# Attention with half-width key and query buffers, a new order of its steps, later weights, and the first layer's first two chunks taken together

## The chip, the cores and the metric

One NeuronCore of one Trainium2 chip runs the whole program in one launch. The metric is the device time in microseconds (us); lower is better. The engines are PE (TensorE matmul, with PEld for its weight loads), DVE (VectorE), ACT (ScalarE), POOL (GpSimd), and SP, which here only issues DMAs. TensorE's clock has two levels, 1.2 and 2.4 GHz; the profile gives the granted clock as a share of the upper one.

## What is computed

```
q, k, v: 4 batches x 8 heads x 576 tokens x 64
scores = q k^T / 8, a key block of 64 seen only by query blocks at or behind it
x   = softmax(scores) v          -> 2304 tokens x 512
x   = (s * relu(x w_in)^2 + b) w_out                 (d_ff 2048)
h   = max(x w1, x w2, x w3)                          (d_ff 768)
out = h w_out2
```

All in fp32; the weights arrive as 64-bit words and are turned into fp32 on the chip.

## The kernel before

The program has one function that records every operation with its reads, writes and a price per engine, and a planner (`Sched.run`) that then writes the instructions out in one fixed order per engine. What the planner puts behind what is settled at build time; on the chip each engine takes its list in order and waits at the head of it. `CFG` holds the tables that steer the planner: `order` (the steps of one round of attention), `pre` (how many weights are converted in each round), `off` (priorities by kind), `eng` (which engines may take a step), and the numbers of buffers.

**Attention** runs in 16 pairs of heads, each pair of one batch. For a pair `load_pair` brings keys and queries (one DMA of 1152 KB) and `load_values` the values. `prep_pair` makes the operands: high part of the keys (`khi`), of the queries (`qhi`), low parts (`klo`, and a fused step of L490), a scaled copy (`q2`), and small tiles for the first query block (`k0`). `softmax_pair` has nine units: scores on PE (full 128x128 array; the first unit on 64x64 tiles), a row maximum on DVE (L524), the exponential on ACT (L528). `values_pair` has five steps, each of which turns the weights of one key block on PE (transposes, L589), copies them out of PSUM on ACT (L389) and multiplies by the values on 128x64 tiles of the array. Round p does the scores of pair p, the values of pair p-1 and the operands of pair p+1. Raw keys and queries have two buffers, one in the tile `other` and one lent from the far end of the result tile `xf`; the staging buffers for weights are two plus two lent.

After the fourth, eighth, twelfth and sixteenth pair the reciprocals of the denominators go to DRAM and come back spread over the partitions (`normalize`, DMA of L796, multiplication of L800 on DVE).

**Weights.** One of w_in or w_out is 512 KB of words. `convert` takes four DVE operations (L694, L702, L706, L711) and one on ACT or POOL, `pair_out` one more on ACT or DVE and one subtraction on DVE (L394). The first half of the first layer's weights (16 tiles, `prepare_direct`) goes straight into SBUF; the others go to DRAM (`wscr`, `bscr`) and are fetched later. Of the 16, `pre` puts 11 into the rounds of attention.

**First layer.** 2304 tokens are cut in five chunks (three of 512, two of 384). A pass takes one chunk and 8 of the 16 blocks of d_ff: `l1` is 12 matmuls and five element steps that give h (relu, square, scale, high and low part), `l2` is 12 matmuls that add to four accumulators. Passes 0 to 4 use the first half of the weights, passes 5 to 9 the second half. The second layer follows.

In all of this a product of fp32 numbers is three matmuls on high and low parts, so one `l1` or `l2` of a block is 12 matmuls. The four lines that make the plan of the passes and of the first weights:

```
PASSES = [(0, c) for c in range(NC)] + [(1, c) for c in reversed(range(NC))]
order1 = [k for f_ in range(HF) for k in [("in", f_)] + [("out", f_ - 1)] * (f_ > 0)] + [("out", HF - 1)]
direct = order1[:8] + [k for k in order1[8:] if k[0] == "in"] + [k for k in order1[8:] if k[0] == "out"]
"pre": (0, 0, 0, 1, 1, 1, 1, 1, 1, 1, 1, 1, 1, 1)
```

Of the kernel before, what the change touches and what calls it, by code (L numbers as in the profile page):

```python
# [20 lines left out]
KT = DM // 128  # L21
# [77 lines left out]
class Ring:  # L99
    def __init__(self, aps):  # L100
        self.aps, self.last, self.n = aps, [None] * len(aps), 0

    def get(self):
        i = self.n % len(self.aps)
        self.n += 1
        u = Use(self.aps[i], [self.last[i]] if self.last[i] else [])
        self.last[i] = u
        return u


# [30 lines left out]


class Both:


    def __init__(self, own, lent):
        self.own, self.lent, self.i = own, lent, 0

    def get(self):
        self.i += 1  # L150
        n = len(self.own.at) + len(self.lent.aps)
        return (self.own if self.i % n < len(self.own.at) else self.lent).get()

    def close(self):

        gone, self.lent.aps = [u for u in self.lent.last if u], []
        for u in gone:
            u.over = True
        return [i for u in gone for i in u.ops]
# [23 lines left out]
class Sched:  # L183
# [45 lines left out]
    def run(self):  # L229
# [26 lines left out]
        while len(order) < n:  # L256
# [28 lines left out]
            if e == "PE":  # L285

                if side and not self.ops[i][5]:
                    c += 54
                side = self.ops[i][5] == "side"
# [11 lines left out]
def tile_attention_moe(ctx: ExitStack, tc: tile.TileContext, qk, vp, w_in, w_out, s_, b_, w123, w_out2, out):  # L301
# [13 lines left out]
    def places(at, n, *sizes):  # L315

        out_ = []
        for m, w in zip(n, sizes):
# [13 lines left out]
    SAT, NAT, at = places(0, (2, 2), 1024, 512)  # L332
    TAT = places(0, (5,), HN)[0]
    RAWAT, K0AT, NMAT, DENAT, RDAT, RVAT, PTAT, *EAT = places(at, (CFG["raw"], CFG["k0"], CFG["nmx"], 2, 1, CFG["rawv"], CFG["pt"]) + tuple(CFG["e"]),
                                                              2 * 2 * S, 256, NB, 36, 128, 17 * D, 1024, *e_w)
    FN = EAT.pop()
    RGAT1, PAT, SAT2, WV2, WB2, UAT, fn = places(at, (3, 4, 4, 2, 4, 6), 512, 512, 1024, 1024, 512, HN)
# [8 lines left out]
    wscr = dram.tile([2 * NF + NG, 128, 1024], F32, name="wscr")  # L346
    pscr = dram.tile([KT, 128, NT], F32, name="pscr")
# [12 lines left out]

    late = xf[:, :, 2 * S:]
    stages = [late[:, 3 - i, 0:1024].rearrange("p (c w) -> p c w", w=2) for i in range(CFG["lent"])]
    raws = [late[:, 0:2, :]] if CFG["lent"] == 2 else []

    def words2(t):
        return t.rearrange("p (c w) -> p c w", w=2)
    rings = dict(raw=Both(Strip(other, RAWAT, 4 * S, two), Ring(raws)), k0=Strip(other, K0AT, 256, lambda t: t[0:64]), nmx=Strip(other, NMAT, NB), den=Strip(other, DENAT, 36),
                 rdt=Strip(other, RDAT, 128), rawv=Strip(other, RVAT, 17 * D, lambda t: t.rearrange("p (a c) -> p a c", c=D)), pt=Strip(other, PTAT, 1024),
                 k1=Strip(arena, kq_at, 1152), q1=Strip(arena, [x + 1152 for x in kq_at], 1024, two), kq2=Strip(arena, [x + 2176 for x in kq_at], 2176),
                 x1=Strip(arena, XAT1, 1024, two), h1=Strip(arena, HAT1, 1024, two), iw=Strip(arena, IAT, 1024, two), ow=Strip(arena, OAT, 1024, two),  # L370
                 x=Strip(arena, XAT, 2 * HN, two), v=Strip(arena, VAT, 1024, two), h=Strip(arena, HAT + HATB, 2 * HN, two), w=Strip(arena, WAT_, 512, two),
                 wb=Strip(other, WB2, 512, two), wv=Strip(other, WV2, 1024, two),
                 stg=Both(Strip(other, SAT, 1024, words2), Ring(stages)), nrm=Strip(other, NAT, 512), rg1=Strip(other, RGAT1, 512), part=Strip(other, PAT, 512), t1=Strip(other, TAT[0:2], HN), t2=Strip(other, TAT[2:4], HN), tt=Strip(other, TAT[4:], HN), y=Strip(other, WV2, 512),
                 u=Strip(other, UAT, HN), rg=Strip(other, RGAT, HN), gb=Strip(other, GAT, HN),
                 **{"e%d" % j: Strip(other, EAT[j], w) for j, w in enumerate(e_w)})
# [23 lines left out]
    def load(size, f, eng="SP", **k):  # L399

        k["after"] = [op(eng, 380, f, lat=2000, **k)]
        return op("DMA", size / 330, lambda e: None, **k)
# [37 lines left out]
    def load_pair(p):  # L440
        b, hp = divmod(p, H // 2)
        R = rings["raw"].get()
# [8 lines left out]
        else:  # L451
            def f(e):
# [892 lines left out]
```

## Time and profile before

| what | value |
|---|---|
| median of 3 runs | 890.1 us (889.54 to 891.33) |
| the profiled execution, its own time | 888.34 us |
| its span, first to last instruction | 886.5 us |
| PE busy | 856.0 us (97%), 4802 matmuls |
| DVE busy | 624.0 us (70%) |
| ACT busy | 444.3 us (50%) |
| POOL busy | 92.6 us (10%) |
| DMA | 166.12 MB, mean 187 GB/s |
| mean granted TensorE clock | 0.985 |

Busy shares are means over stages with different limits: attention lasts to about 213 us, the first layer to about 600 us, the second to the end. Matmuls are pipelined, so a busy PE may still be waiting inside a matmul; the time from one matmul's start to the next tells more than the busy time.

### The profile page before, as it was taken

To read this page: it belongs to the slowest core of one execution; us is meant where nothing else is said; L and a number is where in the kernel's file an instruction comes from. 1 tells how busy PE (TensorE), PEld (TensorE's weight loads), DVE (VectorE), ACT (ScalarE), POOL (GpSimd) and SP (SyncE) were. 2 spreads that over 40 slices of the span, in tenths; PEclk is the share of its full clock that TensorE was granted. 3 is DMA by queue.
4 is the path that set the end of the run, shared out by engine and by line. 5 is a ranking of instruction groups with operands and counts; after the bars stand their busy time and mean duration, and the time that the engine had idled before them with its cause. 6 is when DMAs were issued, how large, how long until landed. Compare 5 with 4: busy or idle time off the path is not lost.

```text
span 886.5 us, 13632 instructions
## 1 busy us (share of the span) xinstructions
PE 856.0 (97%) x4802; PEld 740.7 (84%) x4802; DVE 624.0 (70%) x1211; ACT 444.3 (50%) x964; POOL 92.6 (10%) x96
## 2 busy tenths in 40 slices
PE   8899898889999999999999999999999999999997
PEld 7666565557788888999999888889999899989996
DVE  6898899887899999984734242546767666756662
ACT  5688887677577777764645343543013211331102
POOL 5332222210211031210000000000000000000000
PEclk9899999899999999999999999999999999999999
DMA  8454365554678988799311010126776477637641
GB/s 323 168 182 153 105 214 176 197 174 149 198 257 299 325 289 302 270 389 370 145 60 48 1 47 1 51 96 223 232 226 203 140 235 226 204 133 254 211 146 72
DMA packets 68755, 166.12 MB, mean 187 GB/s; under 512 B 8144, under 2 KB 12496, under 8 KB 67152
## 3 DMA queue, kind: packets, MB, share of 16 engines
q1 hardware_dynamic: 68000, 164.54, 54.9%
q8 instruction: 38, 0.62, 0.3%
q10 hardware_dynamic: 688, 0.72, 0.2%
q14 instruction: 29, 0.24, 0.1%
HBM read 127.67 MB, written 37.56 MB: 186 GB/s over the span
## 4 chain that ended last, share of the span: by engine, by line
PE 70%; DVE 13%; DMA 6%; ACT 6%; issue 3%; POOL 1%; SPq 0%; DVEq 0%; ACTq 0%; POOLq 0%
PE ps L397 67%; PE ps L589 3%; DMA other<-scr 3%; ACT other L528 3%; DVE arena L394 2%; DVE other L524 2%; DMA wscr<-other 2%; DVE other L711 2%; DVE other L394 2%; DVE other L706 1%; DMA bscr<-other 1%; POOL other L385 1%; ACT other L381 1%; DVE other L702 1%; DVE other L694 1%
## 5 line engine op out<-in xcount | busy, mean ns | idle before, releaser
L397 PE MATMUL ps<-arena 128*128 128x384 f32 (+6 forms) x3758 | 747.5, 357 | 9.3 <-ACT other L528 5.8
L397 PEld LDWEIGHTS ps<-arena 128*128 128x128 f32 (+1 forms) x3758 | 664.8, 190 | 85.4 <-issue 11.2
L882 DVE TENSOR_TENSOR other<-ps,other 128x384 f32<-128x384 f32 x189 | 101.0, 554 | 64.2 <-PE ps L397 62.4
L394 DVE TENSOR_TENSOR arena<-other,arena 128x384 fp32r<-128x384 f32 (+2 forms) x165 | 108.5, 665 | 18.9 <-ACT arena L381 14.8
L381 ACT ACTIVATE arena<-other 128x384 fp32r<-128x384 f32 (+4 forms) x105 | 61.1, 589 | 89.9 <-DVE other L1214 54.8
L931 ACT ACTIVATE other<-ps 128x512 f32<-128x512 f32 (+1 forms) x80 | 44.2, 552 | 116.1 <-PE ps L397 115.9
L383 DVE TENSOR_SCALAR arena<-other 128x512 fp32r<-128x512 f32 (+3 forms) x68 | 30.7, 452 | 94.8 <-ACT other L943 91.0
L528 ACT ACTIVATE other<-ps,other 128x320 f32<-128x320 f32 (+3 forms) x144 | 78.5, 552 | 33.2 <-DVE other L524 32.9
L389 ACT ACTIVATE other<-ps 128x512 f32<-128x512 f32 (+1 forms) x131 | 67.8, 559 | 29.1 <-PE ps L397 18.2
L524 DVE TENSOR_REDUCE other<-ps 128x1 f32<-128x320 f32 (+3 forms) x144 | 69.4, 513 | 15.0 <-PE ps L397 13.1
L589 PE MATMUL ps<-ident,other 128*128 128x128 f32 x400 | 64.6, 295 | 13.0 <-ACT other L528 6.7
L385 POOL TENSOR_SCALAR other<-other 128x512 f32<-128x512 f32 (+1 forms) x45 | 45.2, 1009 | 264.6 <-DVE other L694 170.3
L894 ACT ACTIVATE other<-ps 128x384 f32<-128x384 f32 x27 | 13.2, 490 | 114.9 <-PE ps L397 94.5
L397 PE MATMUL ps<-other 128*64 128x64 f32 (+5 forms) x640 | 66.7, 330 | 1.6 <-ACT other L389 1.6
L589 PEld LDWEIGHTS ps<-ident,other 128*128 128x128 f32 x400 | 47.2, 148 | 25.1 <-ACT other L528 10.5
L381 ACT ACTIVATE other<-other 128x256 fp32r<-128x256 f32 (+3 forms) x99 | 51.0, 524 | 29.3 <-DVE other L694 18.5
L943 ACT ACTIVATE other<-other,cst 128x512 f32<-128x512 f32 (+1 forms) x80 | 61.8, 772 | 2.0
L397 PEld LDWEIGHTS ps<-other 128*64 128x64 f32 (+1 forms) x640 | 30.2, 139 | 28.0 <-issue 16.1
L936 ACT ACTIVATE other<-other 128x512 f32<-128x512 f32 (+1 forms) x80 | 47.1, 589 | 2.1
L394 DVE TENSOR_TENSOR arena<-xf,arena 128x384 fp32r<-128x384 f32 (+4 forms) x61 | 40.5, 683 | 6.0 <-ACT arena L381 4.0
L394 DVE TENSOR_TENSOR other<-other 128x256 fp32r<-128x256 f32 (+1 forms) x85 | 41.8, 502 | 2.2 <-ACT other L381 1.8
L706 DVE SCALAR_TENSOR_TENSOR other<-other 128x512 uint32<-128x512 uint32 x54 | 39.2, 726 | 5.4 <-POOL other L385 3.3
(45 smaller groups left out, 360.2 us busy)
## 6 DMA issues: line engine op xcount, KB each, us to landing
arena<-bscr SPq DMA_DIRECT2D x189, 256.0 KB, 3.0
bscr<-other SPq DMA_DIRECT2D x63, 256.0 KB, 4.1
other<-qk SPq DMA_DIRECT2D x12, 1152.0 KB, 5.8
wscr<-other SPq DMA_DIRECT2D x22, 512.0 KB, 4.1
arena<-wscr SPq DMA_DIRECT2D x22, 512.0 KB, 5.0
other<-w_out SPq DMA_DIRECT2D x21, 512.0 KB, 5.4
other<-w SPq DMA_DIRECT2D x18, 512.0 KB, 5.5
other<-vp SPq DMA_DIRECT2D x16, 544.0 KB, 4.0
```

The costliest lines, as they stand in the source:

```text
L381: nc.scalar.activation(out=dst, in_=src, func=AF.Copy, scale=m)
L385: nc.gpsimd.tensor_scalar(out=dst, in0=src, scalar1=m, scalar2=1.0, op0=ALU.mult, op1=ALU.mult)
L389: nc.scalar.activation(out=dst, in_=src, func=AF.Copy)
L394: eng[e].tensor_tensor(out=dst, in0=a, in1=b, op=ALU.subtract)
L397: nc.tensor.matmul(o, l, r, start=start, stop=stop)
L524: nc.vector.tensor_reduce(out=NM.ap[:, u:u + 1], in_=v, axis=AX.X if n <= 512 else AX.XY, op=ALU.max, negate=True)
L528: nc.scalar.activation(out=ev, in_=v, func=AF.Exp, bias=NM.ap[:, u:u + 1], scale=1.0, accum_out=DEN.ap[:, d:d + 1])
L589: nc.tensor.transpose(TB.ap[:, 128 * i:128 * i + 128], x, ident)
L706: nc.vector.scalar_tensor_tensor(out=lo_w, in0=hi_w, scalar=3, in1=lo_w, op0=ALU.logical_shift_left, op1=ALU.bitwise_or)
L882: nc.vector.tensor_tensor(out=out_.ap, in0=bank.ap[:, 0:HN], in1=u.ap, op=ALU.add)
L936: nc.scalar.activation(out=r, in_=r, func=AF.Square)
L943: nc.scalar.activation(out=r, in_=r, func=AF.Identity, scale=s_t, bias=b_t)
```

## The change

- **Half buffers.** Keys and queries of a pair each get a buffer of half the width, four in all, in `other`, and a DMA of their own (576 KB). Nothing is lent from `xf` any more; weights have one staging buffer during attention, six after it.
- **A new order.** `values_pair` is split in two: the transposes with their copies (a to e) and the products (A to E). Products and the first score unit, which run on parts of the array, are collected and put out together where the order has a bar: two groups per round. Each of the five turned tiles has one buffer of its own. The planner is told 93 and 55 or 100 ns for a step between the full array and parts of it, where it was told 54 for one direction.
- **Engines.** `khi` and `qhi` go to POOL alone, `q2` to DVE alone, the copies of the result (`je`) to ACT alone. Loads and the normalization are given longer times in the plan.
- **Weights later.** Three weights instead of 11 are converted during attention (rounds 11 to 13); the w_in tiles come first, then the w_out tiles in the order 6, 7, 0 to 5.
- **First two chunks together.** `l1` runs for chunks 0 and 1 and all eight blocks first, then `l2` for both, with eight accumulators. h of blocks 0 to 5 (12 tiles of 512 KB) goes to DRAM (`hscr`) and comes back (`l1_back`). The passes then start at chunk 2.

```
-        R = rings["raw"].get()
+        R = [rings["raw"].get() for _ in range(2)]
...
-                nc.sync.dma_start(out=R.ap, in_=qk[b, hp])
-            load(1179648, f, writes=[(R, (i,) + k) for i in range(2) for k in ALL])
+                nc.sync.dma_start(out=R[i].ap, in_=qk[b, hp, :, i])
+                load(589824, f, lat=2000 if p < 3 else CFG["dlat"], writes=[(R[i], k) for k in ALL])
...
+    def side_by_side():
+        if side:
+            def f(e, fs=[x[1] for x in side]):
+                for g in fs:
+                    g(e)
+            op("PE", sum(x[0] for x in side), f, reads=[r for x in side for r in x[2]], writes=list(dict.fromkeys(w for x in side for w in x[3])),
+               kind="av", mode="side")
+            for g in after_side:
+                g()
...
-    PASSES = [(0, c) for c in range(NC)] + [(1, c) for c in reversed(range(NC))]
+    PASSES = [(0, c) for c in range(2, NC)] + [(1, c) for c in reversed(range(NC))]
...
+    late_ = [HF - 2, HF - 1] + list(range(HF - 2))
+    direct = [("in", f_) for f_ in range(HF)] + [("out", f_) for f_ in late_]
...
+    split_x(1, "x1b")
+    for f_ in range(HF):
+        while ("in", min(f_ + 2, HF - 1)) not in ready:
+            prepare_direct("w")
+        for c in range(2):
+            l1(c, f_, banks.get(SETS[0]), f_ < HF - 2)
+    accs[0, 0], accs[0, 1] = (accumulators(SETS[1 - c], KT) for c in range(2))
+    split_x(2)
+    for i, f_ in enumerate(late_):
+        while ("out", late_[min(i + 2, HF - 1)]) not in ready:
+            prepare_direct("w")
+        for c in range(2):
+            for k in range(KT):
+                l2(c, f_, k, accs[0, c], 0, i)
+        if i + 2 < HF:
+            for c in range(2):
+                l1_back(c, late_[i + 2])
...
-       "order": "1a5b7v06c3428dep",
+        'order': '2ba40AB7c6v|15dCeDEp8|3',
...
-       "pre": (0, 0, 0, 1, 1, 1, 1, 1, 1, 1, 1, 1, 1, 1),
+        'pre': (0, 0, 0, 0, 0, 0, 0, 0, 0, 0, 0, 1, 1, 1),
...
-       "nlat": 4000,
+        'nlat': 9000,
```

`l1_back` is one DMA from `hscr` into the next of the four h buffers.

Where rows move: PE in an early round of attention. Operations with `64x` are on parts of the array (`64x64 x2` first: the first score unit), `128x128` with `ident` are the transposes, the others with `arena` the scores. Before:

```order
L397 MATMUL ps<-other 64x512 x2
L397 MATMUL ps<-other 64x384 x2
L397 MATMUL ps<-other 64x64 x2
L397 MATMUL ps<-arena 128x448 x2
L589 MATMUL ps<-ident,other 128x128 x4
L397 MATMUL ps<-arena 128x320 x4
L397 MATMUL ps<-arena 128x192 x2
L397 MATMUL ps<-other 64x256 x2
L589 MATMUL ps<-ident,other 128x128 x3
L397 MATMUL ps<-arena 128x288 x4
L589 MATMUL ps<-ident,other 128x128 x4
```

and in the changed kernel:

```order
L367 MATMUL ps<-other 64x64 x2
L367 MATMUL ps<-other 64x512 x2
L367 MATMUL ps<-other 64x384 x2
L367 MATMUL ps<-arena 128x192 x2
L561 MATMUL ps<-ident,other 128x128 x7
L367 MATMUL ps<-arena 128x288 x4
L367 MATMUL ps<-arena 128x448 x2
L367 MATMUL ps<-arena 128x320 x2
L367 MATMUL ps<-other 64x256 x2
L367 MATMUL ps<-other 64x128 x2
L367 MATMUL ps<-other 64x64 x10
```

The products of 256, 128 and 64 columns, each on its own between full-array work before, now stand in one block; most rounds have exactly these two blocks.

DVE in the fifth round, before: two weights are under way (L694, L702, L706) among the maxima (L524) and the operands (L383, L394, L490).

```order
L694 TENSOR_SCALAR other<-other 128x512
L524 TENSOR_REDUCE other<-ps 128x1 x4
L702 TENSOR_SCALAR other<-other 128x512
L694 TENSOR_SCALAR xf<-xf 128x512
L706 SCALAR_TENSOR_TENSOR other<-other 128x512
L524 TENSOR_REDUCE other<-ps 128x1 x2
L383 TENSOR_SCALAR arena<-xf 128x1024
L391 COPY xf<-ps 128x64
L394 TENSOR_TENSOR arena<-xf,arena 64x1152
```

and in the changed kernel in a round as early (L353 is `q2`, L364 `klo`, L496 the maxima, L462 the fused step):

```order
L353 TENSOR_SCALAR arena<-other 64x1024
L364 TENSOR_TENSOR arena<-other,arena 64x1152
L496 TENSOR_REDUCE other<-ps 128x1
L462 SCALAR_TENSOR_TENSOR arena<-other,arena 64x1024
L496 TENSOR_REDUCE other<-ps 128x1 x8
```

The weights and the copies are gone from these rounds; nine maxima and three operand steps are left.

SP in the first layer of the changed kernel, where h comes back (L962) among loads of later weights (L680), the normalization (L786) and stores of converted weights (L722). The kernel before has no such rows.

```order
L962 DMA arena<-hscr 128x1024
L680 DMA other<-w_out 128x1024
L680 DMA other<-w_in 128x1024
L962 DMA arena<-hscr 128x1024
L786 DMA other<-scr 64x384 x2
L722 DMA wscr<-other 128x1024
L680 DMA other<-w_out 128x1024
L786 DMA other<-scr 64x384 x2
L962 DMA arena<-hscr 128x1024 x2
L722 DMA wscr<-other 128x1024
```

A return of h stands behind loads and stores that wait for DVE's conversions.

## Rows read from the trace of the kernel before

**Rows 1.** Busy time by stretch: us, then busy us (instructions) of each engine, clock, DMA.
```profile
79.00:213.30 134.30, 117.79 (x901) 79.11 (x900) 114.08 (x204) 101.86 (x286) 25.70 (x29) 0.95 0.50 168
240.00:880.00 640.00, 639.62 (x3262) 585.18 (x3262) 420.92 (x856) 267.14 (x481) 29.18 (x20) 1.00 0.57 190
```

**Rows 2.** PE in order of time (start, us, operation): marks of four rounds and the end.
```profile
20.03 1.49 PE L397 MATMUL ps<-other 64*64 64x64 f32 x8
...
36.97 1.99 PE L397 MATMUL ps<-other 128*64 128x512 f32 x12
...
208.45 2.15 PE L397 MATMUL ps<-other 128*64 128x512 f32 x12
...
213.21 0.96 PE L397 MATMUL ps<-arena 128*128 128x512 f32 x3
```

**Rows 3.** Busy time by stretch: three single rounds of attention, columns as in rows 1.
```profile
48.10:58.00 9.90, 9.90 (x84) 6.86 (x83) 9.52 (x17) 8.98 (x29) 4.28 (x4) 1.00 0.49 174
...
58.00:69.20 11.20, 11.20 (x95) 8.41 (x94) 10.81 (x18) 9.61 (x31) 4.75 (x5) 1.00 0.63 203
...
166.30:181.80 15.50, 14.49 (x95) 9.03 (x94) 11.54 (x23) 11.91 (x32) 2.93 (x4) 0.86 0.53 173
```

**Rows 4.** PE in order of time inside the first of these rounds.
```profile
54.44 0.66 PE L589 MATMUL ps<-ident,other 128*128 128x128 f32 x4
55.02 0.55 PE L397 MATMUL ps<-other 128*64 128x128 f32 x8
55.54 0.66 PE L589 MATMUL ps<-ident,other 128*128 128x128 f32 x4
55.96 0.65 PE L397 MATMUL ps<-arena 128*128 128x448 f32 x2
```

**Rows 5.** Instruction groups on DVE and POOL, 37 to 208.5 us: busy, mean ns | idle before.
```profile
L524 DVE TENSOR_REDUCE other<-ps 128x1 f32<-128x576 f32 x28 | 21.0, 750 | 3.9 <-PE ps L397 2.8 <-ACT other L528 0.9
...
L524 DVE TENSOR_REDUCE other<-ps 128x1 f32<-128x448 f32 x28 | 17.3, 618 | 0.9 <-PE ps L397 0.7
...
L394 DVE TENSOR_TENSOR arena<-other,arena 64x1152 fp32r<-64x1152 f32 x10 | 14.2, 1422 | 0.0
L490 DVE SCALAR_TENSOR_TENSOR arena<-other,arena 64x1024 fp32r<-64x1024 f32 x11 | 13.5, 1223 | 0.3
...
L524 DVE TENSOR_REDUCE other<-ps 128x1 f32<-128x320 f32 x28 | 12.9, 484 | 1.4 <-PE ps L397 1.3
...
L385 POOL TENSOR_SCALAR arena<-other 128x1152 fp32r<-128x1152 f32 x10 | 12.4, 1244 | 47.6 <-DMA other<-qk 26.2 <-PE ps L397 14.0 <-issue 7.4
...
L524 DVE TENSOR_REDUCE other<-ps 128x1 f32<-128x192 f32 x27 | 9.4, 348 | 5.1 <-PE ps L397 5.0
...
L385 POOL TENSOR_SCALAR arena<-other 64x1024 fp32r<-64x1024 f32 x4 | 5.9, 1480 | 0.0
```

**Rows 6.** SP, DVE, POOL and PE in order of time, the second and third round's data.
```profile
10.84 0.68 SPq L453 DMA_DIRECT2D xf<-qk  x1
...
23.50 2.25 DVE L383 TENSOR_SCALAR arena<-xf 128x1024 fp32r<-128x1024 f32 x2 [4.73 <-DMA xf<-qk]
...
23.58 1.62 POOL L385 TENSOR_SCALAR arena<-xf 128x1152 fp32r<-128x1152 f32 x1 [6.02 <-PE ps L397]
...
27.32 1.28 PE L397 MATMUL ps<-arena 128*128 128x320 f32 x4 [2.93 <-ACT other L528]
```

**Rows 7.** DVE in order of time: a normalization that waits for its DMA.
```profile
88.60 1.12 DVE L800 TENSOR_TENSOR xf<-xf,other 128x512 f32<-128x512 f32 x1 [2.53 <-DMA other<-scr]
```

**Rows 8.** Start of the first layer: busy time by stretch, DVE and PE groups, one PE wait.
```profile
213.30:300.00 86.70, 84.77 (x373) 69.87 (x374) 80.11 (x148) 61.74 (x99) 12.22 (x11) 1.00 0.76 261
...
L711 DVE SCALAR_TENSOR_TENSOR other<-other 128x512 uint32<-128x512 uint32 x22 | 15.5, 705 | 0.1
...
225.86 1.43 PE L397 MATMUL ps<-arena 128*128 128x512 f32 x5 [1.93 <-DVE arena L394]
```

**Rows 9.** DMA issues of the whole run: count, KB each, median us from issue to landing.
```profile
arena<-wscr SPq DMA_DIRECT2D x22, 512.0 KB, 5.0
```

More of the change, by code (lines that the diff above doesn't have):

```diff
@@ L140, in get @@
         return u
[L143 to L159, printed above, removed]
 class Banks:
@@ L285, in run @@
             if e == "PE":
-                if side and not self.ops[i][5]:
-                    c += 54
-                side = self.ops[i][5] == "side"
+                m = self.ops[i][5]
+                if side != (m == "side"):
+                    c += 93 if not side else 55 if m == "turn" else 100
+                side = m == "side"
             done[i], on[i], end[i], free[e] = True, e, t + c, t + c
@@ L612, in f @@
                 copy_to(e, xf[:, hp, t0 + tok:t0 + tok + n], O.ap[:, src])
-            op({x: y(n) for x, y in (("ACT", c_act), ("DVE", c_dve)) if x in CFG["je"]}, 0, f, reads=[O],
-               writes=[(XF, (hp, b, tok))], after=borrowed if b > 1 else (), kind="jc")
+            after_side.append(lambda: op({x: y(n) for x, y in (("ACT", c_act), ("DVE", c_dve)) if x in CFG["je"]}, 0, f, reads=[O],
+                                         writes=[(XF, (hp, b, tok))], kind="jc"))
         def tile_of(i, h, k):
@@ L644, in unit @@
                 put(TB, o, 0)
-        return [lambda k=k: unit(k) for k in range(5)]
+        return [lambda k=k: turned(k) for k in range(5)], [lambda k=k: product(k) for k in range(5)]
+    side, after_side = [], []
+    def side_by_side():
[7 more added lines that the diff above has]
+                g()
+            side.clear()
+            after_side.clear()
     SCR = Use(scr)
@@ L681, in tile_attention_moe, with convert @@
     VAT_ = {key: i for i, key in enumerate(VNAMES)}
-    def convert(src, kind):
+    def convert(src, kind, after=()):
         G = rings["stg"].get()
@@ L954, in l1, with f, l1_back, l2 @@
         op(CFG_E("hlo", DVE=c_dve(n), Pool=c_pooltt(n)), 0, f, reads=[R, (Hh, 0)], writes=[(Hh, 1)], kind="h", lock=True)
+        if not away:
+            hs[c, f_] = Hh
+            return
+        def f(e):
+            nc.sync.dma_start(out=hscr[HF * c + f_].rearrange("p (a c) -> p a c", a=2)[:, :, 0:n], in_=f32(Hh.ap[:, :, 0:n]))
+        load(1024 * n, f, reads=[(Hh, 0), (Hh, 1)], writes=[(HS, (c, f_))], kind="hf")
+    def l1_back(c, f_):
+        n = CHUNKS[c][1]
+        hs[c, f_] = u = rings["h1"].get()
+        def f(e):
+            nc.sync.dma_start(out=f32(u.ap[:, :, 0:n]), in_=hscr[HF * c + f_].rearrange("p (a c) -> p a c", a=2)[:, :, 0:n])
+        load(1024 * n, f, reads=[(HS, (c, f_))], writes=[(u, 0), (u, 1)], kind="hf")
     PS = Use(pscr)
-    def l2(c, f_, k, accs, part):
+    def l2(c, f_, k, accs, part, i=None):
         c0, n = CHUNKS[c]
         W, Hh, A = ready["out", f_], hs[c, f_], accs[k]
-        i = f_ % (NF // 2)
+        i = f_ % (NF // 2) if i is None else i
         t = slice(c0, c0 + n)
```

245 lines of the change are left out of this document (123 added, 122 removed).

## The prediction, before the run

> **What bounds the kernel now.** I read the busy time by stretch first. From 240 to 880 us PE is busy 639.62 of 640.00 us at full clock: both layers are PE's work laid end to end [rows 1]. The change neither adds nor drops a matmul there, so this stretch can only lose. Attention is the part that can give: from 79 to 213.3 us no engine is full, PE 117.79, DVE 114.08 and ACT 101.86 of 134.30 us, and the clock is granted at 0.95 of 2.4 GHz, so that about a tenth of the stretch ran at 1.2 GHz [rows 1].
>
> Next, PE in order of time, for the length of a round: from the first large product of one round to that of the next. It begins with 20.03 and 36.97 us, and 14 rounds later stands at 208.45; PE goes over to the first layer at 213.21 [rows 2]. So the first round took 16.9 us and the 14 behind it 171.5 us, 12.25 on average. Single rounds differ widely: 9.90, 11.20 and 15.50 us [rows 3]. In the shortest one PE is busy for all of 9.90 us, DVE for 9.52 and ACT for 8.98, at full clock: three engines near their limit at once. In the longest, PE is busy 14.49 us at a clock of 0.86, DVE only 11.54 and ACT 11.91: that round is lost to waiting from one engine to the next and to the slower clock that came with it.
>
> What makes rounds long has three visible causes. Eleven weights are converted in the rounds, five DVE steps each, one of them at 0.705 us [rows 8], among the maxima for which ACT and PE wait. The normalization stands in DVE's fixed order too early: at 88.60 us DVE waited 2.53 us for its DMA [rows 7], and everything behind it waited as well. And at the start keys and queries of the third pair, issued at 10.84 us, were not there before 23.50: they stood behind four or five weight loads in the DMA queue; DVE waited 4.73 us, PE stopped for 2.93 us before 27.32 [rows 6].
>
> **The change, part by part.**
>
> *Products in two blocks.* In the shortest round PE goes four times from the full array to parts of it and back, eight steps; with two blocks it is four. What a step costs is bounded in the same round [rows 4]: four transposes and then a product on parts take 55.02 - 54.44 = 0.58 us to the product's start, four transposes and then a score on the full array 55.96 - 55.54 = 0.42. The difference, 0.16, bounds a step from above; below, nothing. I take 0.10, since the second stretch begins behind such a step and holds part of one itself. Four steps fewer: 0.4 us a round (0 to 0.64).
>
> *Weights out of the early rounds.* Eight weights leave the rounds. Without them a round's DVE work is, by the groups' durations [rows 5], twice (0.750 + 0.618 + 0.484 + 0.348) = 4.40 for eight maxima, 1.42 for `klo`, 1.22 for the fused step, and `q2`, at most as long as that, 1.22: 8.3 us with the maximum of the first unit left out, against 9.52 in a round that PE filled. DVE no longer sets the pace if nothing else holds it up. `khi` and `qhi` are 1.24 and 1.48 us on POOL [rows 5], which is otherwise idle. ACT loses those two and gains the rest of the result copies; it was at 8.98 of 9.90 us with a weight's step in it [rows 3]. I cost these moves at nothing: the cover is PE's 9.5 us; without it the round is ACT's, about 9.0, or DVE's.
>
> So a round without weights is the shortest round less the steps: 9.9 - 0.4 = 9.5 us. Eleven of the 14 I put there; the last three, with a weight each, at 11.2, like the second of the three [rows 3].
>
> *The start.* Without weight loads ahead of them, the third pair's halves come early enough that DVE's 4.73 us and PE's 2.93 us go, with the slow clock behind them. I take 11.2 us for the first round in place of 16.9 (bounds: 9.5 and 16.9).
>
> *The normalization* is planned 5 us later; its multiplications stay. That is inside the 9.5 and 11.2 us above.
>
> *End of attention.* 20.0 + 11.2 + 11 x 9.5 + 3 x 11.2 + 4.8 (the last stretch, kept [rows 2]) = 174.1 us, against 213.2: 39.1 us less.
>
> *The first layer.* A matmul of 512 columns takes 84.77 / 373 = 0.227 us there [rows 8]. A block of d_ff for both chunks is 24 of them, 5.45 us, and wants one new weight; 13 of 16 weights are left when it starts. In the same stretch before, 22 weights were finished in 86.7 us [rows 8], one in 3.94 us, with PE held up once, for 1.93 us behind an operand on DVE. Demand is therefore below what DVE has shown, though DVE stays nearly full (80.11 of 86.70 us). Twelve tiles of h go out and come back, 12.6 MB, but the stores of converted weights of that stretch mostly move behind it; the queue carried 261 GB/s there at a share of 0.76. A returning tile is first asked for when its buffer is free and is wanted 24 + 12 matmuls later, 8.2 us; the fetch of a weight of the same size lands after 5.0 us [rows 9]. That leaves 3.2 us for what stands ahead of it in SP's list. I take 5 us of new waits (six steps of 0.8; bounds 0 and 20), less the 1.93 us that need not come again: +3.
>
> *Sum.* 886.5 - 39.1 + 3 = 850.4 us of span; 1.8 us lie outside it (888.34 - 886.5), which gives 852.2; the profiled execution was 1.8 us under the median of the runs, so **854 us**. One measurement here can tell about 0.2%, 1.8 us, from no change.
>
> **Rivals.**
>
> *POOL in DVE's way.* At 23.50 us two copies on DVE took 2.25 us while POOL's copy of keys beside them took 1.62 [rows 6], against POOL's mean of 1.24 for the same shape [rows 5]: each held up the other. Every round now has both of POOL's large steps beside DVE's operand steps. If they go in turn, a round is 8.3 + 1.24 + 1.48 = 11.0 us, 1.5 more than forecast, in all rounds: 39.1 - 15 x 1.5 = 16.6 saved, 854 + 22.5 = 876 us. Against it: the maxima, more than half of DVE's work, were not stretched in any group [rows 5]. Chance 0.16. The Trainium skill, page "SBUF — State Buffer", section "Who interferes with whom", states that DVE operations with two operands in SBUF, and its fast copies, share a port pair with GpSimd that is locked for a whole instruction, while a reduction never contends. By that rule `klo`, the fused step and `q2` would queue with POOL but the maxima would not; rows 6 agree with the first half.
>
> *The return of h is late.* Six steps of the second half of the two-chunk phase each wait for two tiles. If each step loses 3 us, because a store that waits for DVE stands ahead of the return, that is 18 us in place of 5: 867 us. For it: DMA share 0.76 and a full DVE. Against: 3.2 us of room each time. Chance 0.08.
>
> *The change does not shorten the rounds.* The waits between engines could stay although weights and steps go, since no engine was full from 79 to 213 us. Then a round keeps 12.25 - 0.4 and only the start gains 5.7: 11.3 us saved, 882 us. Against it: 9.90 us was reached once with everything the new round still holds and a weight's step besides. Chance 0.08.
>
> *Slower: weights late.* This one mechanism lies in the first layer. Eleven weights were ready when it began, now three. If each of the other 13 takes w us, PE waits 13 x (w - 5.45). It eats the net gain of 36 us from w = 8.2 on, twice the measured 3.94 us [rows 8]; at 9 us it is 46 us, 854 - 5 + 46 = 895 us. For it: h of both chunks now comes twice as densely, 2.7 us apart, on ACT and DVE, which also convert. Against: DVE did 22 weights in 86.7 us beside the steps of h that 373 matmuls make and use. Chance 0.04.
>
> **How the numbers follow.** The forecast has 0.64. Its own spread: rounds at 9.0 and 10.0, and no new wait, give 854 - 5.5 - 3.6 - 5 = 840; rounds at 9.9 and 8 us more in the first layer give 866. The range, 840 to 876, adds the late return and half of POOL's case; outside lie the other half of that, the unshortened rounds and the slower case, about 0.2. Faster by over 0.2%: 0.94 (all but the slower case and 0.02 between it and the third rival); the same 0.02; slower 0.04.
>
> **What would show it.** Right: round marks 9 to 10 us apart for most of attention, DVE clearly under PE there, two blocks of products per round, the first-layer matmuls starting near 174 us with a clock of 1.00 before them, and no idle of PE over 1 us behind that. Wrong: rounds near 11 us with `klo` and `q2` well over 1.42 and 1.22 us on average (POOL); PE idle released by the DMA from `hscr` (return of h); PE idle in the first 90 us of the layer released by the subtraction on DVE (weights); rounds over 11 us with every engine below nine tenths (the waits stayed). The forecast fails most simply if rounds are no more regular than before.

## The result and the profile after

The changed kernel takes 864.19 us (median of 4 runs, 862.98 to 866.67), beside 890.61 us for the kernel before on the same chip: a ratio of 0.9708, 95% interval 0.9684 to 0.9732. It is faster. The gain is 10 us smaller than forecast (854 us), and the time lies inside the range (840 to 876 us).

First the busy time by stretch, changed kernel (columns as in [rows 1]: us, busy us and instructions of PE, weight load, DVE, ACT, POOL, then clock, DMA share, GB/s): the start, two single rounds, most of attention, the first layer's first 86.7 us, and the time after a wait that is spoken of below.

```profile
0.00:37.00 37.00, 28.98 (x180) 25.02 (x181) 23.55 (x38) 19.60 (x56) 15.87 (x28) 0.82 0.59 191
...
50.40:60.00 9.60, 9.60 (x89) 7.37 (x89) 8.18 (x13) 8.88 (x29) 2.46 (x3) 1.00 0.60 180
60.00:69.90 9.90, 9.68 (x88) 7.34 (x90) 8.79 (x15) 9.01 (x28) 2.94 (x3) 1.00 0.50 172
...
79.00:183.50 104.50, 101.58 (x888) 74.96 (x885) 100.42 (x168) 96.37 (x293) 25.14 (x28) 1.00 0.63 204
...
183.50:270.20 86.70, 83.60 (x363) 68.44 (x361) 67.47 (x129) 50.50 (x85) 8.44 (x8) 0.98 0.84 289
...
247.00:250.90 3.90, 3.84 (x10) 3.02 (x11) 1.29 (x3) 0.00 (x0) 0.00 (x0) 0.56 1.03 420
```

Against [rows 1], PE's share of attention went from 88% to 97% (101.58 of 104.50) at a clock of 1.00 in place of 0.95; a round is like the shortest of before [rows 3], with DVE at 8.2 to 8.8 us in place of 9.5 to 10.8.

PE in order of time, changed kernel: the first score unit, the warm-up matmuls behind it (nothing uses their result), then the marks that answer to [rows 2].

```profile
10.24 0.48 PE L367 MATMUL ps<-other 64*64 64x64 f32 x4 [3.83 <-ACT other L351]
10.65 7.99 PE L367 MATMUL ps<-arena 128*128 128x256 f32 x45
...
29.82 1.99 PE L367 MATMUL ps<-other 64*64 64x64 f32 x12
...
40.41 1.99 PE L367 MATMUL ps<-other 64*64 64x64 f32 x12
...
180.60 2.98 PE L367 MATMUL ps<-other 128*64 128x512 f32 x36
...
183.55 6.63 PE L367 MATMUL ps<-arena 128*128 128x512 f32 x28
```

| us | before | predicted | after | after less predicted |
|---|---|---|---|---|
| first mark | 20.03 | 20.0 | 29.82 | +9.8 |
| first round | 16.94 | 11.2 | 10.59 | -0.6 |
| 14 rounds | 171.48 | 138.1 | 140.19 | +2.1 |
| last mark to first layer | 4.76 | 4.8 | 2.95 | -1.9 |
| both layers to the end of the span | 673.3 | 676.3 | 678.9 | +2.6 |
| span | 886.5 | 850.4 | 862.4 | +12.0 |

So the rounds came as forecast; most of what is missing was lost at the start, where nothing was expected to change. A line of PE at a mark can begin with the score unit, as the one at 20.03 us before does; counted from the large products themselves, the 14 rounds took 139.9 us, and that count is used for all kernels below. The marks are also not quite the same place in the work. Added up over PE's matmuls, the columns that they have passed are 27392 at the first large product now and 25088 before; at 27392 columns the changed kernel is 8.5 us late, not 9.8.

**Why the start is late.** ACT, DVE and SP in order of time, changed kernel, first 8 us; and below, what SP's DMAs waited for from 0 to 12 us (us in all, times, longest).

```profile
0.74 3.13 SPq L420 DMA_DIRECT2D other<-qk  x2
...
6.81 0.36 DVE L353 TENSOR_SCALAR arena<-other 128x384 fp32r<-128x384 f32 x1 [3.38 <-DMA other<-qk]
...
6.78 1.28 ACT L351 ACT_TABLE_LOAD   x1 [6.78 <-DMA other<-qk]
```

```profile
SPq L420 <- DMA other<-qk: 2.3, 1, 2.3
```

The first pair comes in two parts, 192 keys and queries per head ahead of the rest. Before, both parts went to the free part of `xf` and were issued one behind the other. Now they go to half buffers in `other`, and there the program makes the second part wait until the first has landed, and the first copy on DVE wait for both. DVE starts that copy at 6.81 us (before at 3.63), ACT loads its table only behind its own wait, PE stops for 3.83 us, and the clock falls: the 45 warm-up matmuls take 7.99 us (before 6.10), and the first 37 us have a mean clock of 0.82 (before 0.86).

**Where the layers lose.** Following both kernels by the columns that PE has passed since the layer began, the changed one is 2.2 us ahead 20 us into the first layer (the wait of [rows 8] is gone), 3.0 behind after 73 us and 4.9 behind after 289 us; nothing changes from there on. The table has 5.6 us: 0.7 of it is only the mark, because before it the kernel before had already done three of the layer's matmuls:

```profile
211.38 0.95 PE L397 MATMUL ps<-arena 128*128 128x512 f32 x3
```

The first loss, in the changed kernel's PE, in order of time:

```profile
241.18 3.02 PE L367 MATMUL ps<-arena 128*128 128x512 f32 x12 [0.24 <-DMA arena<-hscr]
247.06 15.26 PE L367 MATMUL ps<-arena 128*128 128x512 f32 x59 [2.86 <-DMA arena<-hscr]
```

PE waits for the second and third return of h, and behind the longer wait runs at a clock of 0.56 for 3.9 us. SP in order of time, and its waits from 228 to 242 us, say why the third return is late:

```profile
228.90 0.34 SPq L680 DMA_DIRECT2D other<-w_in  x1
...
231.25 0.38 SPq L962 DMA_DIRECT2D arena<-hscr  x1
...
232.82 0.52 SPq L962 DMA_DIRECT2D arena<-hscr  x1
...
239.35 2.17 SPq L962 DMA_DIRECT2D arena<-hscr  x2
```

```profile
SPq L680 <- DVE arena L364: 6.8, 3, 5.0
...
SPq L962 <- DMA other<-w_in: 1.1, 1, 1.1
```

The load of a weight waited 5.0 us for a staging buffer that DVE had to free, so that SP issued nothing from 224 to 228.9 us; then twelve transfers were issued in nine microseconds. A return also waits for the eighth DMA before it in the program, whose semaphore it takes over; for the third one that was a weight's load, and cost 1.1 us. By PE's steps the third return's buffer was free near 235 us; it was issued at 239.35.

The second loss, 1.7 us, comes between 217 and 271 us into the layer. DVE waited there for the store of a converted weight of the second layer (`bscr`), and PE then for DVE; the wait shown is 0.57 us of it:

```profile
444.56 0.30 DVE L353 TENSOR_SCALAR other<-other 128x256 fp32r<-128x256 f32 x1 [1.07 <-DMA bscr<-other]
```

```profile
446.99 73.37 PE L367 MATMUL ps<-arena 128*128 128x384 f32 x332 [0.57 <-DVE arena L364]
```

### The profile page after: what moved, and what is told of

Read it like the earlier page. It is cut to its first block, busy times and chain, and to the rows that moved or that the text cites. A ratio compares the mean times of both kernels' runs of the same rounds, so it can differ in the third digit from the quotient of the medians.

```text
span 862.4 us, 13770 instructions
## 1 busy us (share of the span) xinstructions
PE 841.5 (98%) x4802; PEld 739.4 (86%) x4802; DVE 613.6 (71%) x1179; ACT 443.6 (51%) x991; POOL 92.5 (11%) x99
## 4 chain that ended last, share of the span: by engine, by line
PE 81%; DVE 9%; DMA 5%; ACT 4%; issue 2%; DVEq 0%; SPq 0%; ACTq 0%
PE ps L367 77%; PE ps L561 4%; DVE arena L364 2%; DMA bscr<-other 2%; DVE other L496 2%; ACT other L500 1%; DMA other<-qk 1%; DVE other L364 1%; DMA arena<-hscr 1%; DMA other<-w_in 1%; DVE other L701 1%; ACT other L351 1%; DVE other L696 1%; DVE other L684 0%; ACT other L359 0%
## 5 line engine op out<-in xcount | busy, mean ns | idle before, releaser
L364 DVE TENSOR_TENSOR arena<-other,arena 128x384 fp32r<-128x384 f32 (+3 forms) x173 | 120.3, 704 | 22.6 <-ACT arena L351 18.4
L351 ACT ACTIVATE arena<-other 128x384 fp32r<-128x384 f32 (+3 forms) x112 | 63.1, 568 | 81.1 <-DVE other L1245 55.2
L359 ACT ACTIVATE other<-ps 128x512 f32<-128x512 f32 (+1 forms) x138 | 73.0, 572 | 43.7 <-PE ps L367 33.6
L924 ACT ACTIVATE other<-ps 128x512 f32<-128x512 f32 (+1 forms) x80 | 44.1, 551 | 99.0 <-PE ps L367 98.9
L353 DVE TENSOR_SCALAR arena<-other 128x512 fp32r<-128x512 f32 (+3 forms) x67 | 36.7, 551 | 74.6 <-ACT other L936 67.9
L500 ACT ACTIVATE other<-ps,other 128x576 f32<-128x576 f32 (+4 forms) x144 | 78.6, 565 | 12.0 <-DVE other L496 11.3
L355 POOL TENSOR_SCALAR other<-other 128x512 f32<-128x512 f32 (+1 forms) x51 | 49.1, 964 | 325.6 <-DVE other L684 190.3
L496 DVE TENSOR_REDUCE other<-ps 128x1 f32<-128x576 f32 (+4 forms) x144 | 68.1, 511 | 15.9 <-PE ps L367 9.0
L561 PE MATMUL ps<-ident,other 128*128 128x128 f32 x400 | 57.7, 281 | 4.7 <-ACT other L500 4.6
L367 PE MATMUL ps<-other 128*64 128x64 f32 (+5 forms) x640 | 55.0, 314 | 3.8 <-ACT other L351 3.8
L364 DVE TENSOR_TENSOR other<-other 128x256 fp32r<-128x256 f32 (+1 forms) x85 | 41.4, 500 | 3.8 <-ACT other L351 3.5
L355 POOL TENSOR_SCALAR arena<-other 128x1152 fp32r<-128x1152 f32 (+4 forms) x31 | 36.1, 1179 | 51.7 <-PE ps L367 34.4
```

What stands on the lines that cost most here:

```text
L351: nc.scalar.activation(out=dst, in_=src, func=AF.Copy, scale=m)
L355: nc.gpsimd.tensor_scalar(out=dst, in0=src, scalar1=m, scalar2=1.0, op0=ALU.mult, op1=ALU.mult)
L359: nc.scalar.activation(out=dst, in_=src, func=AF.Copy)
L364: eng[e].tensor_tensor(out=dst, in0=a, in1=b, op=ALU.subtract)
L367: nc.tensor.matmul(o, l, r, start=start, stop=stop)
L496: nc.vector.tensor_reduce(out=NM.ap[:, u:u + 1], in_=v, axis=AX.X if n <= 512 else AX.XY, op=ALU.max, negate=True)
```

## The experiments

Each kernel differs from the changed one by the edit shown or named. "Layers" is the span less the end of attention. The kernel before, run again beside each of them, took 888.6 to 890.6 us (medians). Where a difference has to reach 2%, e2, e3 and e4 count as the same as the kernel before and e5 as unclear; the others are faster. One execution of each kernel is profiled. In all seven kernels that leave the rounds as the change has them (the changed one, e1 and e7 to e11) the 14 rounds took 139.8 to 140.0 us, so differences of one microsecond can be read there.

| kernel | median us | ratio to before, 95% | attention ends | 14 rounds | layers |
|---|---|---|---|---|---|
| changed | 864.19 | 0.9708 [0.9684, 0.9732] | 183.5 | 139.9 | 678.9 |
| e1_first_pair_apart | 861.67 | 0.9683 [0.9653, 0.9713] | 177.8 | 139.9 | 679.4 |
| e2_products_split | 876.15 | 0.9850 [0.9822, 0.9877] | 197.4 | 152.3 | 676.5 |
| e3_weights_early | 874.26 | 0.9828 [0.9801, 0.9856] | 187.9 | 143.6 | 683.9 |
| e4_engines_shared | 878.25 | 0.9867 [0.9833, 0.9901] | 195.1 | 151.7 | 681.8 |
| e5_chunks_apart | 879.28 | 0.9845 [0.9774, 0.9916] | 182.7 | 138.7 | 695.1 |
| e6_norm_early | 868.82 | 0.9723 [0.9659, 0.9787] | 184.6 | 140.3 | 681.9 |
| e7_return_free | 865.88 | 0.9697 [0.9639, 0.9755] | 184.9 | 139.9 | 679.8 |
| e8_start_and_return | 861.61 | 0.9653 [0.9594, 0.9712] | 178.7 | 140.0 | 681.5 |
| e9_return_early | 865.41 | 0.9730 [0.9708, 0.9753] | 184.6 | 139.9 | 679.3 |
| e10_both_early | 858.43 | 0.9656 [0.9634, 0.9678] | 177.5 | 139.9 | 679.1 |
| e11_second_layer_later | 856.42 | 0.9640 [0.9618, 0.9663] | 176.9 | 139.8 | 676.5 |

**The start.**

```
+            own = R
+            R = [Use(xf[:, i, 2 * S:]) for i in range(2)]
+            for u, w in zip(own, R):
+                u.ops = w.ops
```

> Against the changed kernel's 864.2 us. Only the first pair's raw keys and queries lie elsewhere (in the result tile, as in the kernel before), so that its second DMAs need not wait for its first; the other buffers are handed on as in the changed kernel. Theory (the start was lost because the second half of the first pair's loads waited for the first half): first score unit near 7 us instead of 10.24, first large product at 20 to 24 us instead of 30.1, total 855 to 858 us. Rival (the start is later because of the new order of the rounds and the slower clock there): first large product within 2 us of 30.1, total 862 to 866 us.

PE in order of time, this kernel:

```profile
7.10 0.33 PE L367 MATMUL ps<-other 64*64 64x64 f32 x4
...
24.09 1.99 PE L367 MATMUL ps<-other 64*64 64x64 f32 x12
...
34.69 1.66 PE L367 MATMUL ps<-other 64*64 64x64 f32 x10
...
177.77 57.41 PE L367 MATMUL ps<-arena 128*128 128x512 f32 x252
```

The first score unit is back at 7.10 us and everything behind it comes 5.7 us earlier, to the end of attention. The place of the first pair is what made the start late. 4 us of the first mark remain, 2.8 at equal columns; the second mark, 34.69, is already earlier than before (36.97). The profiled spans differ by 5.2 us, the medians by 2.5, and the intervals overlap; the 855 to 858 us forecast for the edit did not come. Two more pairs of kernels further down differ by this edit alone: e8_start_and_return is 4.3 us faster than e7_return_free, and e10_both_early 7.0 us faster than e9_return_early.

**What shortened the rounds.** Three kernels undo one cause each. First, products and score unit in many blocks again:

```
-        'order': '2ba40AB7c6v|15dCeDEp8|3',
+        'order': '2ba40|A|B|7c6v15dC|eD|E|p83',
```

> Against the changed kernel's 864.2 us. The products stand in the order each on its own again, all else as changed; the list of PE has 110 steps between the full array and parts of it in place of 64 (128 in the kernel before). Theory (a step costs about 0.10 to 0.16 us, and PE sets the rounds): 46 steps make 4.6 to 7.4 us, total 868 to 872 us. Rival (rounds are shorter only because weights left them; the blocks do nothing): total 862 to 866 us. Second rival (the blocks matter by their place, not by their steps, and the list now has better covers): faster than 862 us.

Then eight weights back in the early rounds:

```
-        'pre': (0, 0, 0, 0, 0, 0, 0, 0, 0, 0, 0, 1, 1, 1),
+        'pre': (0, 0, 0, 1, 1, 1, 1, 1, 1, 1, 1),
```

> Against the changed kernel's 864.2 us. Eight weights are converted in rounds 3 to 10 in place of three in rounds 11 to 13. Theory (a weight's DVE steps lengthen a round by some 1.2 to 1.7 us): about eight long rounds in place of three or four, 5 to 8 us more in attention, 0 to 3 us given back in the first layer, total 866 to 872 us. Rival (DVE has room beside 8.3 us of its own work in a round of 9.7): rounds unchanged, total 861 to 865 us.

Then the lists of engines of before:

```
-'khi': ['Pool'], 'klo': ['DVE'], 'q2': ['DVE'], 'qhi': ['Pool']},
+'khi': ['ACT', 'Pool'], 'klo': ['DVE'], 'q2': ['ACT', 'DVE', 'Pool'], 'qhi': ['ACT', 'DVE', 'Pool']},
...
-        'je': ['ACT'],
+        'je': ['ACT', 'DVE'],
```

> Against the changed kernel's 864.2 us. Operands may go to ACT, DVE and POOL again, and result copies to ACT and DVE, as in the kernel before. Theory (POOL alone for the high parts is covered, PE sets the rounds): rounds within 0.3 us of 9.7, total 862 to 870 us, rather slower since ACT is near its limit. Rival (POOL's and DVE's shared work holds the rounds): rounds shorter by 0.3 us or more, total under 860 us.

Busy time over the 14 rounds, columns as above: the kernel before, the changed kernel, e2_products_split, e3_weights_early, e4_engines_shared; then a stretch of e2_products_split.

```profile
36.97:208.45 171.48, 153.49 (x1190) 104.98 (x1190) 152.71 (x264) 135.42 (x391) 41.97 (x45) 0.96 0.49 164
```

```profile
40.67:180.60 139.93, 136.77 (x1190) 102.30 (x1187) 129.49 (x214) 129.72 (x399) 35.18 (x41) 1.00 0.63 201
```

```profile
42.15:194.48 152.33, 145.27 (x1187) 106.37 (x1186) 131.66 (x218) 130.81 (x394) 44.08 (x44) 0.99 0.57 186
```

```profile
41.27:184.87 143.60, 136.81 (x1192) 102.54 (x1188) 137.09 (x228) 130.75 (x398) 41.56 (x46) 1.00 0.63 204
```

```profile
40.40:192.13 151.73, 142.50 (x1195) 105.83 (x1192) 126.95 (x217) 136.12 (x403) 27.25 (x35) 0.99 0.57 184
```

```profile
180.90:184.40 3.50, 3.50 (x15) 3.41 (x16) 2.68 (x6) 2.51 (x8) 0.00 (x0) 0.51 0.93 357
```

What PE's busy time leaves of the stretch is its idle time: 18.0 us before, 3.2 in the changed kernel.

The grouped products are worth 12.4 us in the rounds. With them split, the order has 55 blocks on parts of the array in PE's list, the changed kernel 32: 46 steps more. 3.9 of the 12.4 us are more idle time of PE (7.1 us in place of 3.2). Another 1.7 us, an estimate, is the half of the 3.4 us that PE ran at 1.2 GHz. The 6.8 us left are 0.15 us for each of the 46 steps, also an estimate, and within the bound of 0.16 from [rows 4]. So the theory's price of a step holds; the time is over its 868 to 872 us by PE's idle time and the slow clock.

The lists of engines are worth 11.8 us in the rounds, 10.7 at equal columns, and neither forecast came. With the work shared out, ten of the large operand steps ran on ACT, which is busy 136.1 us over the rounds in place of 129.7, while most of the result copies stayed there. PE was idle for 9.2 us in place of 3.2 and ran 3.4 us at 1.2 GHz. So most of what is lost are waits from one engine to the next, and the clock behind one of them. The two lists, for operands and for copies, were put back together, and no run separates them.

The weights are worth only 3.7 us in the rounds, eight of them against three. All of it is idle time of PE (6.8 us in place of 3.2), and DVE, busy 137.1 of 143.6 us, is the engine nearest its limit. Not undone by any run are the half buffers, the separate buffers of the turned tiles, the planner's new prices and its new priorities (`off` in `CFG`).

With the weights early, the layers are 5.1 us longer, where up to 3 us less was expected, and so the time is over the 866 to 872 us of the theory. PE in order of time in e3_weights_early, the stretch around it, and ACT's step that PE waited for:

```profile
239.03 35.86 PE L367 MATMUL ps<-arena 128*128 128x512 f32 x144 [7.36 <-ACT arena L351]
```

```profile
231.30:244.70 13.40, 5.94 (x14) 3.98 (x13) 13.37 (x26) 6.34 (x10) 2.11 (x2) 0.62 0.58 187
```

```profile
238.28 0.70 ACT L351 ACTIVATE arena<-other 128x512 fp32r<-128x512 f32 x1 [3.35 <-DVE other L701]
```

PE waits there for ACT, and ACT for L701, the last step of a weight's conversion on DVE, which is busy throughout (13.37 of 13.40). So a weight of the first layer came too late here although more of them were early; why the plan put it so late stays open.

**The first two chunks together.**

```
-    PASSES = [(0, c) for c in range(2, NC)] + [(1, c) for c in reversed(range(NC))]
+    PASSES = [(0, c) for c in range(NC)] + [(1, c) for c in reversed(range(NC))]
...
-    direct = [("in", f_) for f_ in range(HF)] + [("out", f_) for f_ in late_]
+    direct = list(order1)
...
-        if n_ or i > 0:
+        if n_ and i % 3 != 2:
...
-CFG = {'aside2': 2,
+CFG = {'aside2': 4,
```

(and the loop over both chunks goes; the last two cuts put the places at which later weights are prepared back to those of the kernel before)

> Undoes only the common first two chunks of the first layer: each chunk goes through all blocks by itself again, h stays in SBUF, weights come in the old order of uses; attention is that of the change. A block is then 24 matmuls of one chunk, 2.7 us, and wants two weights (in and out), or one per 12 matmuls, while weights were made at one in 3.94 us. Theory (the common phase is what lets the weights be late): PE waits for weights through the first chunk; 13 late weights at 3.94 - 2.7 = 1.2 us each are 16 us of waits, 880 us in all; bounds 872 and 895. Rival (weights would be in time anyway, the round trip of h costs and brings nothing): no waits over 1 us and the 5.5 us of the first layer go: 858 to 860 us.

PE in order of time, then the groups of DVE's last step of a weight in the first 86.7 us of the layer (busy, mean ns), first here and then in the changed kernel:

```profile
202.59 10.44 PE L367 MATMUL ps<-arena 128*128 128x512 f32 x36 [8.72 <-ACT arena L351]
215.61 0.73 PE L367 MATMUL ps<-arena 128*128 128x512 f32 x2 [2.58 <-ACT arena L351]
```

```profile
L701 DVE SCALAR_TENSOR_TENSOR other<-other 128x512 uint32<-128x512 uint32 x26 | 17.8, 687 | 0.1
```

```profile
L701 DVE SCALAR_TENSOR_TENSOR other<-other 128x512 uint32<-128x512 uint32 x18 | 12.8, 713 | 0.2
```

The layers are 16.2 us longer, as the theory had it (16). By columns this kernel is 17.1 us behind the changed one 40 us into the layer: the two waits shown take 11.3 us, and from 182.7 to 226 us the mean clock is 0.84. It is 11.8 behind after 91 us, when the changed kernel has had its own loss, and 17.5 after 217 us, behind smaller waits for ACT and DVE that may belong to the places of the later weights. So the waits for the first weights are as large as the theory has them; that the sum at the end meets it so closely is in part chance. It is the common phase, with its one weight per 5.45 us, that lets the weights be late; without it the layers lose half of what the rounds won. A block of 24 matmuls also takes 5.45 us with the chunks apart, but wants two weights, one per 2.7 us (the expectation gives the 2.7 to the whole block). Even at 26 weights in 86.7 us (3.3 us each) DVE is too slow for that.

**The normalization.** Its plan as before (`nlat` 4000, one step).

> Undoes only the later planning of the normalization (its planned delay from 9000 back to 4000, its DMA one step again). Theory (small part of the gain): DVE waits again for the normalization's DMA, 1 to 2.5 us at a few places, some of it passed to PE: 14 rounds at 141 to 145 us in place of 139.9, 865 to 869 us. Rival (the later plan is what made the rounds regular): rounds of 11 us and more, over 875 us.

The rounds stay at 140.3 us, under the 141 forecast; the layers lose 3.0. DVE in order of time in this kernel, where PE then waited 1.11 us, and 1.23 us behind a second such wait:

```profile
203.18 0.56 DVE L790 TENSOR_TENSOR xf<-xf,other 128x384 f32<-128x384 f32 x1 [1.40 <-DMA other<-scr]
```

The theory holds in kind, at another place than forecast. By columns only 1.0 us against the changed kernel is left of these waits 73 us into the layer; the other 2 us come between 250 and 271 us. The runs (863.94 to 870.49) spread too far to give the size.

**The return of h.** First without the preparations in the loop (`prepare_aside` dropped there), then that and the start together:

> Leaves out the four preparations of later weights that stand in the loop where h returns; they come behind it. Theory (the first returns of h wait because SP's list and the DMA queue hold those loads and stores before them): PE's wait of 3.25 us and the half clock for 3.4 us behind it go, 859 to 861 us. Rival (the queue is full of attention's own transfers and normalization's reads then, the loads do not matter): the waits stay at 3 to 5 us in sum, 863 to 866 us. A third way: the later weights are then late in the next chunk, and new waits stand there.

> The first pair's keys and queries come into a place of their own, and the preparations are out of the loop in which h returns: the two edits together. If the two gains add, the start gives 2.5 us (what it gave alone) to 5.7 us (by the marks in its trace), the return 3 to 5: 855 to 859 us. If the return's waits only move: 861 us, as with the start's edit alone.

PE in order of time, e7_return_free:

```profile
245.15 7.32 PE L367 MATMUL ps<-arena 128*128 128x512 f32 x24 [2.89 <-DMA arena<-hscr]
253.55 8.70 PE L367 MATMUL ps<-arena 128*128 128x512 f32 x37 [1.08 <-DMA arena<-hscr]
```

This theory fell: the waits are as long, so it is not those four preparations alone. What stays ahead of the returns are the normalization's reads and the weights of the loop itself. So the return was moved instead:

```
+                 hx=Strip(arena, XAT1[0:2], 1024, two),
...
-    split_x(2)
+    for c in range(2):
+        l1_back(c, late_[2], "hx")
     for i, f_ in enumerate(late_):
+        if i == 3:
+            split_x(2)
...
-        if i + 2 < HF:
+        j = i + 3 if i < 2 else i + 2
+        if i != 2 and j < HF:
```

> Only the return of h: the first block comes back into two operand buffers that the first chunk has left free, before the second product of the layer begins, the next two blocks are asked for one step (5.45 us) earlier than in the change, and the operands of the third chunk are made after the third step in place of before the first. Theory (what PE waits for is the place of the return in SP's list and the seven transfers in flight before it, not the transfer itself): the waits of 0.62 and 3.25 us at 240 to 247 us and the half clock for 3.4 us behind them go, 4 to 5.5 us less: 859 to 861 us. Rival (the DMA engines are the limit there: some 4 MB have to pass at about 400 GB/s before PE can go on, whatever their order): the wait moves to a weight or a later return, 862 to 866 us.

> The return as in e9_return_early, and the first pair's keys and queries in a place of their own as in e1_first_pair_apart. If both gains add: attention's end at 177.8 us, layers at 668 to 670 us, 855 to 858 us. If the return's waits only move, 861 us as the start's edit alone gave.

PE in order of time, e9_return_early:

```profile
264.89 3.06 PE L367 MATMUL ps<-arena 128*128 128x512 f32 x12 [1.00 <-DMA arena<-hscr]
```

The waits at 240 to 247 us and the slow clock are gone, and smaller ones stand later; 91 us into the layer this kernel is 2.7 us ahead of the changed one. But 271 us into it, it is level again: the gain is lost between 402 and 456 us. In time the edit alone brings nothing (865.41 us), as its rival had it. With the start's edit the median is 858.43 us against 861.67, but the two profiled spans are only 0.6 us apart, and the layers, at 679.1 us, are not at the 668 to 670 that would show both gains. In e10_both_early ACT, in order of time, shows the later place:

```profile
428.57 0.44 ACT L351 ACTIVATE other<-other 128x256 fp32r<-128x256 f32 x1 [2.49 <-DMA bscr<-other]
```

ACT waited for the store of a weight of the second layer, with a step of h behind it in its list, and PE then for ACT. So those weights begin one chunk later (`'aside2': 3` in place of 2):

> e10_both_early, and the preparation of the second layer's weights begins one chunk later (the third of the remaining passes in place of the second counts as its start). In e10_both_early the layers lost 4 us against the kernel before between 413 and 449 us, where ACT waited 2.5 us twice for the store of such a weight with a step of h behind it in its list. Theory (it is their density there): these waits go, layers at 669.5 to 671 us, 854.5 to 857 us. Rival (a later weight is then late, or the waits belong to the first layer's own weights): 858 us or more.

PE in order of time, then one stretch of this kernel:

```profile
176.86 70.99 PE L367 MATMUL ps<-arena 128*128 128x512 f32 x312
...
261.32 78.81 PE L367 MATMUL ps<-arena 128*128 128x512 f32 x385 [0.84 <-DMA arena<-hscr]
```

```profile
240.00:270.00 30.00, 28.00 (x121) 22.26 (x120) 17.31 (x32) 7.70 (x13) 1.78 (x2) 1.00 0.98 356
```

The loss between 217 and 271 us into the layers shrank from 3.9 to 1.9 us, the layers by 2.6 us to 676.5 (not to the 669.5 to 671 forecast), and the kernel takes 856.42 us: faster than before and, by 0.7% with the three edits together, than the change, whose interval lies clear of this one's. The intervals of this kernel and of e10_both_early overlap. What is left of the return's waits stands in a stretch with the DMA engines busy 0.98 of it, which speaks for the rival there: the transfers themselves.

## Why the prediction was right, and where not

*What bounds it: right.* PE was the limit of the layers and the waits between engines that of attention; PE is now busy 97% of attention.

*A round of 9.5 us: right in sum, wrong in its parts.* 14 rounds took 140.2 us against 138.1. The working had it from the weights (out of DVE's way) and 0.4 us of steps, and said of the engines "I cost these moves at nothing". Undone one by one, grouped products are worth 12.4 us, the engines 11.8 and the weights 3.7, 27.9 of the 31.6 us between 171.5 and 139.9, though effects found one at a time need not add. The price of a step lay in its bounds (0.10 us taken, some 0.15 measured). What the working did not see is how much of the waits and of the slow clock came with the old order and the old lists of engines, and how little with the weights. The forecast held because it took the shortest round as the measure of one without mishaps, not because it had the reasons' sizes.

*The start: the step that failed.* The sum took "20.0" as kept, and its part on the start looked only at the third pair, where the gain came: 10.6 against 11.2 us. That the first pair moves to another buffer stood in the change, and the order of SP's list with its waits would have shown the second DMA behind the first. It cost 9.8 us at the first mark, 8.5 at equal columns; e1_first_pair_apart gave back 5.7. That the time still lies in the range is in part luck: the upper part of the range was made for a late return and for POOL, not for the start.

*First layer, +3: mis-sized.* It came to +5.6 us, 0.7 of it from the mark. The return was late once, by about 3 us and the slow clock after it, not at six steps by 0.8. So one of the prediction's own signs, no idle of PE over 1 us, failed, and the sign of the rival with a late return was there, at a sixth of its 18 us. Another 1.7 us come after 200 us of the layers, which the allowance left out; there DVE waited for the store of a weight of the second layer, and beginning those conversions later took 2 us from the same place (e11_second_layer_later against e10_both_early).

*POOL in DVE's way: the mechanism is there, the price is not.* DVE and POOL in order of time, changed kernel:

```profile
57.05 1.33 DVE L364 TENSOR_TENSOR arena<-other,arena 64x1152 fp32r<-64x1152 f32 x1
...
65.64 2.18 DVE L364 TENSOR_TENSOR arena<-other,arena 64x1152 fp32r<-64x1152 f32 x1
...
54.42 2.16 POOL L355 TENSOR_SCALAR arena<-other 128x1152 fp32r<-128x1152 f32 x2 [3.56 <-PE ps L367]
...
63.98 2.65 POOL L355 TENSOR_SCALAR arena<-other 128x1152 fp32r<-128x1152 f32 x2 [3.56 <-PE ps L367]
```

`klo` took 1.33 to 1.35 us in the eight rounds in which POOL had finished, 2.18 to 2.20 in the four in which the last 0.98 us of POOL's step lay in it; `q2` likewise took 0.68 us or up to 1.53, and POOL's pair of steps 2.16 or up to 2.65. The one waits for the other, as the Trainium skill, page "SBUF — State Buffer", section "Who interferes with whom", states for these kinds of operation. The delays of `klo` and `q2` add up to some 8 us in 12 rounds, 0.7 us a round where the rival had 1.5, and they cost PE nothing visible: DVE has 8.2 to 8.8 us of work in a round, these delays included, and PE is busy for all of the round of 9.60 us. Sharing the work out again (e4_engines_shared) was 14 us slower, not faster.

*Weights late: rightly left at a small chance.* One weight in 4.8 us (18 in 86.7) was enough for one wanted every 5.45. The reason is the common phase, as e5_chunks_apart shows.

## What to carry to other kernels

Take the shortest of many like rounds as the measure of what a round can be, but find its reasons by undoing one cause at a time: here an assignment of engines that was costed at nothing was worth as much as the grouping. When a buffer moves, read what its first use waits for, above all at the very start, where nothing covers it. Look also at what stands ahead of a transfer that PE will wait for in the list that issues it: here one stalled prefetch held it up, and then the burst behind that. But a wait that is removed is not yet time won: with the return moved ahead, its wait and the slow clock were gone and the time was the same; a later place gave the gain away again.

## What was not expected of the hardware

PE's wait of 2.86 us was followed by 3.4 us at 1.2 GHz; the one of 7.36 us in e3_weights_early came with 10.2 us at it (234.5 to 244.7), 5.7 of them behind the wait. Waits of up to 0.84 us between 247 and 262 us in e11_second_layer_later left the clock at 2.4. So, by an estimate from halving the speed, the two long waits cost their own length and 0.6 and 0.4 of it again. The length of one wait does not settle it: PE's wait of 1.22 us before 180.85 us in e2_products_split came with the 3.4 us at 1.2 GHz shown above, and one of 1.22 us before 178.71 us in the changed kernel left the clock at 2.4.
